# Weight signs from a two-slope ReLU on ScalarE, and a sum-of-squares bound for the weights, in an attention and MLP kernel

## The chip, the cores and the metric

The kernel runs on one core of one Trainium2 chip. The metric is the device time of one execution in microseconds (us). The core has a TensorE (PE; its weight loads are shown apart as PEld), a VectorE (DVE), a ScalarE (ACT), a GpSimd (POOL) and a SyncE (SP) that issues most of the DMAs.

## The reference

Attention over 4 batches of 8 heads, 768 positions of 64 numbers, in which a query sees only the keys of its own hash bucket; then a two-layer MLP with the ELU function between its layers. The MLP's weights reach the kernel as 64-bit floating-point numbers.

```python
q_bucket = np.sum((einsum(q, proj) > 0) * 2**arange(6), -1)      # k_bucket likewise
scores = np.where(q_bucket == k_bucket, q @ k.T / 8, -1e9)
attn = exp(scores - max) ; attn /= attn.sum() + 1e-9
x = (attn @ v)                      # 3072 tokens x 512
h = x @ w_in                        # w_in 512 x 2048
g = np.where(h > 0, h, exp(min(h, 0)) - 1)
out = g @ w_out                     # w_out 2048 x 512
```

## The kernel before

**Numbers in two halves.** Each matrix product runs on 16-bit operands. A 32-bit tensor is scaled by a power of two and split into a high half (helper `scaled`, line 143 when ScalarE does it) and the remainder (helper `rest`, line 152, on VectorE). Three matmuls then stand for one product: high by high, high by low and low by high. The power of two comes from a bound on the tensor, which `powers` (line 174) turns into an exponent `ex` and a scale `sc`. With `rows=True` the bound is already the same on each partition; without it, `powers` first adds the partitions up with a small matmul against the matrix `ones`, into a PSUM tile of pool `ps_a` (line 184). With `squares=True` the bound is a sum of squares, whose exponent is halved (lines 191 to 194, two VectorE instructions where the plain way has one, line 196).

**Weights.** `w_in` and `w_out` make 32 tiles of 128 x 512, 16 each. `wload` (line 444) loads a tile as pairs of 32-bit words (512 KB) into a ring of three places in `U` and one at the end of `W`. `wdecode` (line 460) makes 32-bit floats of it. The upper word `hi` of a 64-bit number, read as a 32-bit float and multiplied by 2^-112 on ScalarE (line 467, recorded at line 143), has its exponent where a shift left by 3 on VectorE (line 468) puts it right; the shift also pushes the sign out. Line 469 (VectorE) brings in three bits of the lower word `lo`. Then a matmul (line 472) of `ones` with the upper 16-bit halves of the tile adds its columns into the PSUM tile `acc`; while the sign is out, these are sums of magnitudes. At last line 479 (VectorE) takes the sign bit from `hi` and puts it in place. After the last tile of each matrix, line 477 reduces `acc` to its greatest entry, `wscale` (line 485) makes the scale, and `wsplit` (line 491) makes the 16-bit halves, which overwrite `W` in place. They are the tiles `w0s` (for `w_in`) and `w1s` (for `w_out`) in the profile.

**Attention.** The work goes by slots: 8 chunks (half a batch each) of 4 head pairs, 6 slots to a pair. A slot is 128 queries of one head against all 768 keys: `scores` (line 504) issues four matmuls and a VectorE instruction (line 520) that copies the scores out of PSUM and takes the maximum of each row; `exps` (line 528) does two slots' exponentials on ScalarE (line 536); `splits` (line 541) makes halves (lines 143 and 152, tile `hl`) and a DMA turns them over (line 551, tile `PT`). After a pair, `attend` (line 553) issues 36 matmuls into a `ps_a` tile, the pool's single buffer, and makes `x16`. `prep_k`, `prep_q` and `prep_v` load, scale and turn over the inputs ahead of their slots.

**MLP.** `moe_stream` (line 575) runs `first` (line 580: twelve matmuls into `h`, line 588, then ELU and the halves of `g`) and `second` (line 610: nine matmuls into `o`, line 624) for each chunk and each of 16 column groups. It can't begin before the first chunk's four `attend` calls and the `w_in` halves.

**What sets the order.** The loop over slots (line 894) issues scores, exponentials, MLP steps, input preparation and up to six weight steps (`weights(W_RATE)`, line 924) for each slot. A weight step is a `wdecode`, a `wsplit` or nothing, if the space of `W` is still in use by early inputs or if a load hasn't been issued. The framework's scheduler then sets each engine's order from its own forecast of times; from slot 30 on (`starts[0]`), TensorE's order is that of the program. Each engine executes its instructions in the order of its queue.

Of the kernel before, what the change touches and what calls it, by code (L numbers as in the profile page):

```python
# [9 lines left out]
BF16 = mybir.dt.bfloat16  # L10
F32 = mybir.dt.float32
I32 = mybir.dt.int32
AF = mybir.ActivationFunctionType
ALU = mybir.AluOpType
# [6 lines left out]
W_TOP = 13  # L21
# [30 lines left out]
    "n_lo": ("V", "V"),  # L52
    "v_hi": ("A", "A"),
    "v_lo": ("V", "V"),
    "w_mul": ("A", "A"),
    "w_sgn": ("V", "V"),
    "w_hi": ("A", "A"),
    "w_lo": ("V", "V"),
    "g_hi": ("A", "A"),
# [7 lines left out]
def lsh_attention_moe(  # L67
# [10 lines left out]
    nc = tc.nc  # L78
# [4 lines left out]
    P = 128  # L83
# [6 lines left out]
    FG = 4  # L90
    SL = FG * P
    NSI = (NF // FG) * KT
    NSO = NF
# [3 lines left out]
    const = ctx.enter_context(tc.tile_pool(name="const", bufs=1))  # L97
# [34 lines left out]
    def engine(kind):  # L132
        rest = int(now[0] > 0)
        n = turns.get((kind, rest), 0)
        turns[kind, rest] = n + 1
        names = ENGINES[kind][rest]
        return names[n % len(names)]

    def scaled(kind, o, x, s):

        e = engine(kind)
        if e == "A":
            nc.scalar.activation(o, x, AF.Copy, scale=s)  # L143
        elif e == "V":
            nc.vector.tensor_scalar(o, x, s, None, ALU.mult)
        else:
            nc.gpsimd.tensor_scalar(o, x, s, 1.0, ALU.mult, ALU.mult)
# [18 lines left out]
    ones = const.tile([P, P], BF16, name="ones")  # L166
# [7 lines left out]
    def powers(mx, n, floor, top, tag, pool=None, rows=False, squares=False, ex=None):  # L174

        pool = pool or small  # L180
        mall = pool.tile([P, n], F32, tag=tag + "m", name=tag + "m")
        if not rows:
            t = ps_a.tile([P, 512], F32, tag="av", name="sum")[:, :n]
            nc.tensor.matmul(t, ones, mx.bitcast(BF16).rearrange("p (n t) -> p n t", t=2)[:, :, 1], start=True, stop=True)
            mx = t
        nc.vector.tensor_scalar(mall, mx, floor, None, ALU.max)
        if ex is None:
            ex = pool.tile([P, n], F32, tag=tag + "e", name=tag + "e")
        if squares:

            nc.vector.tensor_scalar(
                ex.bitcast(I32), mall.bitcast(I32), 1, 0x7F800000, ALU.logical_shift_right, ALU.bitwise_and
            )
            nc.vector.tensor_scalar(ex, ex, 2.0**64, None, ALU.mult)
        else:
            nc.vector.tensor_scalar(ex.bitcast(I32), mall.bitcast(I32), 0x7F800000, None, ALU.bitwise_and)
        sc = pool.tile([P, n], F32, tag=tag + "s", name=tag + "s")
        nc.vector.reciprocal(sc, ex)
        nc.vector.tensor_scalar(sc, sc, 2.0**top, None, ALU.mult)
        return ex, sc  # L200
# [226 lines left out]
    wst = {}  # L427
# [32 lines left out]
    def wdecode(i):  # L460

        t = w64.pop(i)
        d = W[:, i + (2 if i >= NSI else 1), :]
        di = d.bitcast(I32)
        lo, hi = t[:, :, 0], t[:, :, 1]

        scaled("w_mul", d, hi.bitcast(F32), 2.0**-112)
        nc.vector.tensor_scalar(di, di, 3, None, ALU.logical_shift_left)
        nc.vector.scalar_tensor_tensor(di, lo, 29, di, ALU.logical_shift_right, ALU.bitwise_or)  # L469

        o = int(i >= NSI)
        nc.tensor.matmul(  # L472
            wst["acc"], ones, d.bitcast(BF16).rearrange("p (n t) -> p n t", t=2)[:, :, 1],
            start=i == o * NSI, stop=i in (NSI - 1, NSI + NSO - 1),
        )
        if i in (NSI - 1, NSI + NSO - 1):
            nc.vector.tensor_reduce(wst["m2"][:, o : o + 1], wst["acc"], axis=AX.X, op=ALU.max)
        if engine("w_sgn") == "V":
            nc.vector.scalar_tensor_tensor(di, hi, -(2**31), di, ALU.bitwise_and, ALU.bitwise_or)
        else:  # L480
            sign = hi.bitcast(F32)
            nc.scalar.activation(sign, sign, AF.Sign)
            nc.gpsimd.tensor_tensor(d, d, sign, ALU.mult)

    def wscale(o):
        wst["ex", o], wst["sc", o] = powers(wst["m2"][:, o : o + 1], 1, 2.0**-17, W_TOP, f"w{o}", const, rows=True)
        if o == 1:
            wst["e2"] = const.tile([P, 1], F32, name="we2")
            nc.vector.tensor_tensor(wst["e2"], wst["ex", 0], wst["ex", 1], ALU.mult)
# [244 lines left out]
    last = {}  # L734
# [3 lines left out]
    for ns in groups:  # L738
# [3 lines left out]
        for n in ns:  # L742
            at = begin[n] - (PREP0 if early else PREP)[2]

            w = 2 * chunks[pairs[n][0]]["nc"]
# [20 lines left out]
        for i, n in enumerate(ns):  # L766
# [7 lines left out]
            last = {"split": a, "project": z_last}  # L774
# [64 lines left out]
    def weights(n):  # L839
        nonlocal w_credit, w_at  # L840
        w_credit += n
        while w_credit >= 1:

            at = (w_at + (2 if w_at >= NSI else 1)) * SL
            users = {x[1] for x in due} | ({"v"} if len(vdue) == NP + 2 + (B - 1) * (2 * NP + 3) else set())
            if any(a < at + SL and at < z and users & u for a, z, u in guards):
                break
            if w_at not in w64 and w_at < NSI + NSO:
                break
            w_credit -= 1  # L850
            if w_at >= W_SPLIT and NSI not in split_done and len(split_done) < KT:
                split_w()
            elif w_at < NSI + NSO:
                wdecode(w_at)
                w_at += 1
                load_w()
                if w_at in (NSI, NSI + NSO):
                    wscale(w_at // (NSI + NSO))
            elif wq and (wq[0] if wq[0] < NSI else (wq[0] - NSI) // FG * KT) // KT <= moe_at[0] // FG + 1:
                split_w()  # L860
            else:
                break
# [31 lines left out]
    for G in range(starts[-2] + 1):  # L894
        if G == starts[0]:
            ordered.enter_context(tc.manual_schedule(engines={mybir.EngineType.PE}))
        if G < len(slots):
            n, at = slots[G]
            c = chunks[pairs[n][0]]
            b, p, j, t = c["b"], pairs[n][1], at // c["nc"], at % c["nc"]  # L900
# [59 lines left out]
```

## Time and profile before

| | before |
|---|---|
| median of 3 runs | 952.3 us (950.54 to 952.47) |
| span of the profiled execution | 952.0 us |
| TensorE busy | 817.4 us, 86% |
| VectorE busy | 703.4 us, 74% |
| ScalarE busy | 741.4 us, 78% |
| GpSimd busy | 15.7 us, 2% |
| mean granted TensorE clock | 0.958 |

A slice row of the profile cuts the span into 40 equal pieces of 23.8 us, and each digit is an engine's busy share in tenths. A row of a group gives the line of the kernel, the engine, the operation, output and input tiles with their shapes, the count, and then the busy time, the mean duration in ns of one, and the idle time of the engine just before such instructions with what ended it. A row of a stretch gives its start and end, its length, each engine's busy time and count, the granted clock (1.00 is full), the DMA engines' mean share and the rate in GB/s. Lines 143 and 152 belong to helpers, so the tile names tell the groups apart. The DMA share adds up the time that packets took, so it can pass 1.

### The profile page before, as it was taken

The numbers are of one execution on the slowest core, as the hardware profiler recorded it, in microseconds if no ns is written. First come the engines' busy times: TensorE is split into PE (matmuls) and PEld (weight loads), VectorE is DVE, ScalarE is ACT, GpSimd is POOL, SyncE is SP. The second block draws the span as 40 slices with busy tenths as digits, with TensorE's granted clock in tenths as the row PEclk, the third lists the DMA queues.
The fourth block names the chain that finished last, engine by engine and source line by source line (L and its number), as shares of the span: only waits on it lengthen the run. The fifth ranks groups of instructions, "written<-read, shape, count | busy, mean of one in ns | idle before, by whom it ended". The sixth has DMA issues, their size and how long they took to land.

```text
span 952.0 us, 14531 instructions
## 1 busy us (share of the span) xinstructions
PE 817.4 (86%) x4975; PEld 420.6 (44%) x4975; DVE 703.4 (74%) x1524; ACT 741.4 (78%) x1473; POOL 15.7 (2%) x49
## 2 busy tenths in 40 slices
PE   2445555987999999988998999998989999999996
PEld 0112222544545555544554455544445555555553
DVE  6798999887877867678776686787877687764332
ACT  5578876988979878789779787889888788885442
POOL 1000000000000000000000000000000000000000
PEclk9998656999999999999999999999999999999998
DMA  9999898676787768687887758795786767556000
GB/s 284 237 225 217 224 252 170 118 142 145 148 164 166 149 113 140 129 184 120 161 182 135 138 110 148 150 185 102 140 148 130 123 118 150 101 100 100 34 1 35
DMA packets 404587, 138.48 MB, mean 145 GB/s; under 512 B 380960, under 2 KB 398880, under 8 KB 404512
## 3 DMA queue, kind: packets, MB, share of 16 engines
q1 hardware_dynamic: 402432, 131.25, 69.5%
q0 software_dynamic: 1920, 6.29, 1.9%
q8 instruction: 39, 0.64, 0.3%
q14 instruction: 36, 0.29, 0.1%
q10 hardware_dynamic: 160, 0.00, 0.0%
HBM read 35.65 MB, written 6.29 MB: 44 GB/s over the span
## 4 chain that ended last, share of the span: by engine, by line
issue 77%; PE 11%; DMA 5%; DVE 3%; ACT 2%; POOL 1%; POOLq 0%; ACTq 0%; DVEq 0%
PE o L624 3%; PE h L588 3%; PE av L559 2%; PE s L508 2%; DMA K<-natk 1%; DMA O<-nat1q 1%; DMA out_dram<-W 1%; POOL out_dram L638 1%; ACT pt L536 1%; DVE pt L520 1%; DVE hl L152 1%; DMA PT<-hl 1%; DMA vf<-in_v_dram 0%; DVE natk L152 0%; ACT hl L143 0%
## 5 line engine op out<-in xcount | busy, mean ns | idle before, releaser
L624 PE MATMUL o<-W,U 128*128 128x512 f16 x1152 | 280.3, 379 | 4.3 <-ACT W L143 4.2
L588 PE MATMUL h<-x,W 128*128 128x384 f16 x1536 | 280.8, 327 | 0.8 <-ACT x L568 0.6
L588 PEld LDWEIGHTS <-W 128*128 128x128 f16 x1536 | 147.7, 98 | 112.6 <-issue 11.9
L536 ACT ACTIVATE pt<-pt,nb,sg 128x768 f32<-128x768 f32 x192 | 195.3, 1019 | 1.7
L152 DVE SCALAR_TENSOR_TENSOR hl<-pt,r,hl 128x768 f16<-128x768 f32 x192 | 189.5, 1012 | 8.8 <-ACT hl L143 8.4
L143 ACT ACTIVATE hl<-pt,r 128x768 f16<-128x768 f32 x192 | 168.4, 926 | 22.4 <-DVE r L546 22.0
L520 DVE TENSOR_SCALAR_CACHE_REDUCE pt<-s 128x768 f32<-128x768 f32 x177 | 168.1, 949 | 21.8 <-PE s L508 20.7
L508 PE MATMUL s<-K,O 128*128 128x384 f16 x708 | 153.8, 341 | 32.1 <-DVE pt L520 31.7
L624 PEld LDWEIGHTS <-U 128*128 128x128 f16 x1152 | 111.0, 98 | 125.4 <-issue 11.7
L559 PE MATMUL av<-PT,vhl 128*64 128x384 f16 x1152 | 113.8, 347 | 27.1 <-DMA PT<-hl 16.7
L603 DVE SCALAR_TENSOR_TENSOR U<-U 128x384 f32<-128x384 f32 x128 | 71.0, 555 | 86.7 <-ACT U L602 85.7
L508 PEld LDWEIGHTS <-O 128*128 128x128 f16 (+1 forms) x768 | 74.9, 102 | 129.9 <-issue 55.0
L152 DVE SCALAR_TENSOR_TENSOR U<-U,sgg 128x384 f16<-128x384 f32 x128 | 78.4, 612 | 59.7 <-ACT U L143 59.7
L599 ACT ACTIVATE U<-h,ch 128x384 f32<-128x384 f32 x128 | 72.9, 569 | 62.5 <-PE h L588 62.3
L559 PEld LDWEIGHTS <-vhl 128*64 128x64 f16 x1152 | 73.0, 116 | 73.5 <-ACT W L143 13.2
L143 ACT ACTIVATE U<-U,sgg 128x384 f16<-128x384 f32 x128 | 77.8, 608 | 19.9 <-DVE U L603 19.8
L602 ACT ACTIVATE U<-h,ch 128x384 f32<-128x384 f32 x128 | 73.0, 570 | 0.0
L472 PE MATMUL acc<-W,ones 128*128 128x512 bf16 x32 | 17.1, 554 | 33.9 <-DVE W L469 33.9
L536 ACT ACTIVATION_READ_ACCUMULATOR pt<-pt,nb,sg 128x1 f32 x192 | 36.3, 189 | 0.0
L533 ACT ACTIVATE nb<-m,sg 128x2 f32<-128x2 f32 x96 | 27.7, 288 | 8.7 <-DVE pt L520 8.7
L207 ACT ACTIVATE nat1q<-qst 128x384 bf16<-128x384 f32 x30 | 15.5, 517 | 18.9 <-DMA O<-nat1q 18.1
L291 DVE TENSOR_SCALAR zb<-z,pjt 64x384 f16<-64x384 f32 (+1 forms) x48 | 29.1, 606 | 1.2 <-PE z L286 1.2
(102 smaller groups left out, 527.2 us busy)
## 6 DMA issues: line engine op xcount, KB each, us to landing
U<-in_moe_w_in_dram SPq DMA_DIRECT2D x12, 512.0 KB
vf<-in_v_dram SPq DMA_DIRECT2D x16, 384.0 KB
U<-in_moe_w_out_dram SPq DMA_DIRECT2D x12, 512.0 KB
out_dram<-W POOLq DMA_DIRECT2D x24, 256.0 KB, 4.0
qst<-in_q_dram SPq DMA_DIRECT2D x30, 192.0 KB
kst<-in_k_dram SPq DMA_DIRECT2D x14, 384.0 KB
PT<-hl SPq DMA_TRANSPOSE x192
W<-in_moe_w_in_dram SPq DMA_DIRECT2D x4, 512.0 KB
```

The lines of the kernel that those rows point to most:

```text
L143: nc.scalar.activation(o, x, AF.Copy, scale=s)
L152: nc.vector.scalar_tensor_tensor(o, x, s, hi, ALU.mult, ALU.subtract)
L291: nc.vector.tensor_scalar(zb[used], t[used], pj["thr"][used, which : which + 1], (MBIT, -MBIT)[which], ALU.is_gt, ALU.mult)
L508: nc.tensor.matmul(s_tile[:, n, :HALF], st[o][:rows, at, :], kst[kk][:rows, j * NC + n * HC : j * NC + (n + 1) * HC, :].rearrange("p a b - ...
L520: top = nc.vector.tensor_scalar(pt.rearrange("p (n e) -> p n e", n=2), s_tile[:, :, :HALF], CLAMP, None, ALU.max, ALU.max, accum_out=duo[0 ...
L536: nc.scalar.activation(pt, pt, AF.Exp, bias=nb[:, n : n + 1], scale=st["sg"][:, 0:1], accum_out=sm[:, n : n + 1])
L559: nc.tensor.matmul(av[j * D : (j + 1) * D], vt[:, j, c, vx, :], PTs[j][:, :, px, c, :], start=n == 0, stop=n == last,)
L588: nc.tensor.matmul(h, WH[:, g * KT + t, wx, fc * P : (fc + 1) * P], c["xs"][t][:, xx, :], start=n == 0, stop=n == 3 * KT - 1,)
L599: nc.scalar.activation(e, h, AF.Exp, scale=c["ch"])
L602: nc.scalar.activation(hp, h, AF.Relu, scale=c["ch"])
L603: nc.vector.scalar_tensor_tensor(e, e, -1.0, hp, ALU.add, ALU.min)
L624: nc.tensor.matmul(o[t][:, :DO], g16[:, gx, t * P : (t + 1) * P], WH[:, NSI + 1 + f, wx, :], start=f == 0 and i == 0, stop=f == NF - 1 and ...
```

## The change

The first step of `wdecode` becomes a ReLU with a slope for negative inputs (`Prelu`). A positive word is multiplied by 2^-112 as before. A negative word is multiplied by 2^-112 and by -(2^32): it comes out positive with an exponent that is greater by 32, and the shift left by 3 moves that bit of the exponent to the place of the sign. So the float has its sign after line 469, and the VectorE instruction of line 479 is gone, and with it the last reading of the upper words after the ScalarE step.

The tile has its signs when the bound is taken, so a sum of the columns no longer bounds it. In place of one matmul of `ones` with 512 columns, each tile now has four matmuls, each of a 128 x 128 block of the upper halves with itself, whose diagonal holds the sums of squares of the block's columns. The maximum over `acc` is taken as before. It differs from partition to partition, so `wscale` calls `powers` without `rows`, which adds the small matmul with `ones` into a `ps_a` tile, and with `squares`, which has one more VectorE instruction. Both happen once for each matrix.

```diff
-    "w_mul": ("A", "A"),
-    "w_sgn": ("V", "V"),
...
-        scaled("w_mul", d, hi.bitcast(F32), 2.0**-112)
+        nc.scalar.activation(d, hi.bitcast(F32), AF.Prelu, scale=2.0**-112, alpha=-(2.0**32))
         nc.vector.tensor_scalar(di, di, 3, None, ALU.logical_shift_left)
         nc.vector.scalar_tensor_tensor(di, lo, 29, di, ALU.logical_shift_right, ALU.bitwise_or)
         o = int(i >= NSI)
-        nc.tensor.matmul(
-            wst["acc"], ones, d.bitcast(BF16).rearrange("p (n t) -> p n t", t=2)[:, :, 1],
-            start=i == o * NSI, stop=i in (NSI - 1, NSI + NSO - 1),
-        )
-        if i in (NSI - 1, NSI + NSO - 1):
+        top = d.bitcast(BF16).rearrange("p (n t) -> p n t", t=2)[:, :, 1]
+        last = i in (NSI - 1, NSI + NSO - 1)
+        for u in range(FG):
+            x = top[:, u * P : (u + 1) * P]
+            nc.tensor.matmul(
+                wst["acc"][:, u * P : (u + 1) * P], x, x,
+                start=i == o * NSI and u == 0, stop=last and u == FG - 1, skip_group_check=True,
+            )
+        if last:
             nc.vector.tensor_reduce(wst["m2"][:, o : o + 1], wst["acc"], axis=AX.X, op=ALU.max)
-        if engine("w_sgn") == "V":
-            nc.vector.scalar_tensor_tensor(di, hi, -(2**31), di, ALU.bitwise_and, ALU.bitwise_or)
-        else:
-            sign = hi.bitcast(F32)
-            nc.scalar.activation(sign, sign, AF.Sign)
-            nc.gpsimd.tensor_tensor(d, d, sign, ALU.mult)
     def wscale(o):
-        wst["ex", o], wst["sc", o] = powers(wst["m2"][:, o : o + 1], 1, 2.0**-17, W_TOP, f"w{o}", const, rows=True)
+        wst["ex", o], wst["sc", o] = powers(wst["m2"][:, o : o + 1], 1, 2.0**-34, W_TOP, f"w{o}", const, squares=True)
```

## The prediction

> **What bounds the kernel now.** I read the page first, its slices above all, then a table of busy time by stretches, whose cuts I chose from the slices.
>
> ```profile
> span 952.0 us, 14531 instructions
> PE   2445555987999999988998999998989999999996
> DVE  6798999887877867678776686787877687764332
> PEclk9998656999999999999999999999999999999998
> ```
> ```profile
> 0.00:40.00 40.00, 10.42 (x39) 2.34 (x39) 26.19 (x89) 20.19 (x38) 2.57 (x25) 1.00 0.99 279
> 40.00:90.00 50.00, 28.36 (x127) 11.05 (x126) 45.76 (x120) 36.95 (x74) 0.00 (x0) 1.00 0.93 218
> 90.00:170.00 80.00, 45.11 (x210) 19.80 (x211) 75.13 (x155) 63.50 (x123) 0.00 (x0) 0.60 0.88 204
> 170.00:260.00 90.00, 79.32 (x489) 41.08 (x488) 76.70 (x166) 81.06 (x162) 0.00 (x0) 0.96 0.74 142
> 260.00:930.00 670.00, 640.39 (x4046) 339.68 (x4045) 475.35 (x991) 533.32 (x1069) 11.52 (x21) 1.00 0.68 129
> ```
>
> In each stretch the columns after its length are PE, PEld, DVE, ACT and POOL busy, then clock, DMA share and rate. The reader is to see two kernels in one span. From 260 to 930 us PE is busy 640.39 of 670: that part lasts as long as TensorE needs, and nothing that the change touches lies in it. Before 170 PE is half idle and DVE is the full engine: 45.76 of 50 and 75.13 of 80. In 0 to 40 DVE has only 26.19 of 40, and the DMA share is 0.99. So what VectorE sheds before 170 is worth time, more in the third stretch than in the first, and every microsecond by which the MLP starts earlier ends the kernel as much earlier. All weight tiles are decoded in that early part:
>
> ```profile
> L588 PE MATMUL h<-x,W x1536: 323/326/527, 169.9 to 937.6; 128*128 128x384 f16 x192
> L624 PE MATMUL o<-W,U x1152: 376/379/634, 179.1 to 943.4; 128*128 128x512 f16 x192
> L469 DVE SCALAR_TENSOR_TENSOR W<-U,W x24: 670/682/693, 13.4 to 157.1; 128x512 int32<-128x512 int32 x24
> ```
>
> The first `h` matmul starts at 169.9 and the last decoding step of line 469 at 157.1.
>
> **Removed: the sign step.** Two groups hold line 479, and the stretches tell where it runs.
>
> ```profile
> L479 DVE SCALAR_TENSOR_TENSOR W<-U,W 128x512 int32<-128x512 int32 x24 | 16.4, 682 | 0.7 <-PE acc L472 0.7
> L479 DVE SCALAR_TENSOR_TENSOR W<-W 128x512 int32<-128x512 int32 x8 | 5.5, 682 | 0.1
> ```
> ```profile
> 0.00:40.00 40.00, 6.14 (x9) 1.00 0.99 279
> 40.00:90.00 50.00, 5.42 (x8) 1.00 0.93 218
> 90.00:170.00 80.00, 10.24 (x15) 0.60 0.88 204
> ```
>
> 32 steps of 682 ns are 21.8 us of VectorE, and that is the most that can be gained. I credit each stretch apart. In 0 to 40 the first attention slots wait for inputs that come by DMA; DVE idles 13.8 us, and a shorter DVE mostly idles longer. Of 6.14 I take 1, with 0 and 4.0 as ends (4.0 is 6.14 by DVE's busy share of 26.19 in 40). In 40 to 90 DVE is 92% busy; of 5.42 I take 3.3. In 90 to 170 it is 94% busy, and the slots' chain runs through it; of 10.24 I take 7, because the DMA share of 0.88 leaves 80 - 70.4 = 9.6 us by which that stretch can shrink before the same packets fill it. Sum: 11.3, ends 0 and the whole 21.8.
>
> What comes late next is the turning over of `hl` (DMA), then `attend`: after line 152's last `hl` of a pair come a transfer and 36 matmuls, and no weight step shortens these. That is why I take two thirds and not all.
>
> **Moved: the ring place comes free sooner.** Line 479 was the last reader of a loaded tile, now it is line 469. The weight loads wait for it on SP's queue, where the transposes stand behind them.
>
> ```profile
> SPq L456 <- DVE W L479: 8.5, 7, 2.8
> DVE W L468 <- ACT W L143: 3.9, 8, 0.8
> DVE zb L291 <- PE z L286: 1.0, 2, 0.7
> DVE W L479 <- PE acc L472: 0.7, 1, 0.7
> PE acc L472 <- DVE W L469: 33.9, 15, 6.5
> ```
>
> Seven loads waited 8.5 us in all for the sign step. They will be issued one VectorE step earlier, 0.7 us or more each. They then meet the transposes a little earlier, in stretches with a DMA share of 0.88 to 0.99. ACT's wait for weights isn't on the path to the slots, so I count 0, with -1 (loads out of the transposes' way) and +2 (in their way) as ends.
>
> **Changed: the scaling step on ScalarE.** The trace has no such ReLU with a slope.
>
> ```profile
> L143 ACT ACTIVATE W<-U 128x512 f32<-128x512 f32 x24 | 15.7, 663 | 14.5 <-DMA U<-in_moe_w_in_dram 7.8 <-DMA U<-in_moe_w_out_dram 6.6
> L143 ACT ACTIVATE W<-W,w0s 128x512 f16<-128x512 f32 x16 | 11.3, 709 | 2.2 <-DVE W L152 2.2
> L602 ACT ACTIVATE U<-h,ch 128x384 f32<-128x384 f32 x128 | 73.0, 570 | 0.0
> L599 ACT ACTIVATE U<-h,ch 128x384 f32<-128x384 f32 x128 | 72.9, 569 | 62.5 <-PE h L588 62.3
> L207 ACT ACT_TABLE_LOAD x1 | 1.3, 1283 | 2.0 <-issue 2.0
> ```
>
> The plain scaling of such a tile takes 663 ns, one whose scale comes from a tile 709; Exp (line 599) and ReLU (line 602) of one shape take 569 and 570, so the function sets no price here. I take 663, hence nothing; the other end is 709, 32 x 46 ns = 1.5 us of an engine that is busy 120.6 of 170 us. Nothing below nothing: the element count is the same. One row more matters: the only table load of the whole trace, 1283 ns. It returns as a rival.
>
> **Changed: the bound.** Per tile one weight load and one matmul of 512 columns become four of each with 128 columns. The trace has no such matmuls, so I go by pace, in three rows: consecutive weight loads of the score matmuls (384 columns each) under a half clock, and two full-clock runs of the MLP.
>
> ```profile
> 157.02 0.15 PEld L508 LDWEIGHTS <-O 128*128 128x128 f16 x1 [0.17 <-issue]
> 157.34 0.15 PEld L508 LDWEIGHTS <-O 76*128 76x128 f16 x1 [0.17 <-issue]
> ```
> ```profile
> 305.51 1.94 PE o L624 x9
> 308.11 1.95 PE h L588 x12
> ```
>
> At full clock 512 columns take 1.94/9 = 0.216 us, 384 take 0.163; at half clock 384 take 0.32, so 512 would take 0.43. Four pairs with a weight load each cost no less than the same 512 columns, and no more than four of the 384 kind: 0.216 to 0.65 us a tile at full clock, 0.43 to 1.28 at half. The extra is 0 to 0.43 and 0 to 0.85. The Trainium skill speaks against the change here: "TensorE: Matmul & The Clock Gate", section "Back-to-back issue gap", puts a stream of loads and matmuls at about 81 ns a matmul for 128 columns and 131 for 512, so by it the estimate is 324 against 131, 0.19 us more a tile; the trace's 0.216 for 512 is not its 131. With all 32 tiles on the path the sum would lose some 6 us by it, an estimate.
>
> What lies beside it: PE is idle 21.6 of 50 and 34.9 of 80 us, much of it in front of this very matmul (33.9 us for line 469). Behind it in PE's queue stand the scores, for which line 520 waits; but the list of DVE's waits before 170 has no wait for scores, and the greatest for PE is 1.0 (line 291). So DVE has scores in hand. I count 1 us on the path. If that cover is gone, the whole extra counts: 17 tiles before 90 us at up to 0.43 and 15 after at up to 0.85, 20.1 us.
>
> **Added: one small matmul and a wait, twice.**
>
> ```profile
> L184 PE MATMUL sum<-vx,ones 128*128 128x1 bf16 x4 | 0.7, 177 | 1.4 <-DVE x L569 1.4
> L194 DVE TENSOR_SCALAR ve<-ve 128x1 f32<-128x1 f32 x4 | 0.6, 146 | 0.0
> ```
> ```profile
> 160.23 0.68 DVE L477 TENSOR_REDUCE wm<-acc 128x1 f32<-128x512 f32 x1
> 163.24 0.15 DVE L186 TENSOR_SCALAR w1m<-wm 128x1 f32<-128x1 f32 x1
> 164.45 4.89 PE L559 MATMUL av<-PT,vhl 128*64 128x384 f16 x35 [0.55 <-DMA PT<-hl]
> ```
>
> The matmul is 177 ns and the instruction 146 ns. The matmul waits for line 477 and for the one `ps_a` buffer; behind it in PE's queue stand scores and `attend`, and `powers` on DVE waits for it. For `w_out` the reduction is at 160.23, line 186 at 163.24: 2.3 us of slack lie between them already. If it lands behind an `attend`, the scale comes up to 4.9 us later; the `w_out` halves aren't read before 179.1. I count 0.3 us, ends 0 and 5.
>
> **Sum.** 11.3 - 1 - 0.3 = 10 us off the span of 952.0, so 942.0. The span is 0.3 below the median of 952.3, so the forecast of the median is 942.3. On the way the scheduler gets other durations and may set another order on DVE and ACT; the trace can't price that, and I let it widen the range by a few us.
>
> **The rivals.** *DVE's gain in full.* If the DMA packets' time is mostly waiting for one another (the share of 0.99 in the first stretch holds 279 GB/s, 0.88 holds 204), DMA yields, and up to 21.8 us go: 930.5. For it: DVE near 94% busy; against: the idle 13.8 us of the first stretch, and the transfers at each pair's end. Chance 0.12 for 935 or less.
>
> *DMA holds the start.* The transposes and loads of 170 us have a share that adds up to 0.99 x 40 + 0.93 x 50 + 0.88 x 80 = 156.5 us. If they can't be packed closer, DVE's freed time turns into waits for `PT` and `K`, and the gain is 2 or less: 950 to 953. Against it: pauses in the share and DVE's few waits for DMA. Chance 0.08.
>
> *TensorE takes DVE's place.* At half clock (0.60 in the third stretch) each decode puts four loads and matmuls ahead of scores, in order. From the point where the extra on the path passes the 0.68 us that DVE saves per tile, the change loses; at the upper price of 0.85 a tile it does. With the whole 20.1 us on the path and the forecast's credit of 11.3: 952.3 + 8.8 = 961. Against it: PE's idle time above. Chance 0.05.
>
> *The slope function isn't in the loaded table.* Then it needs one table load, and the next Exp one back. If it happened for each of 32 tiles, 64 x 1.283 = 82 us of ACT; it has 170 - 120.6 = 49 free, so at least 33 us are over: about 975 with the credit of 10, and more with less. Once per few tiles would still eat ScalarE's slack. One load in this trace serves squares, Copy, Exp and ReLU. The Trainium skill, "ScalarE: Activation LUTs", section "Table sets: the hidden batching unit", names relu, copy and abs as filler in every set, and doesn't name this function; no run here shows it yet. Chance 0.03.
>
> **How the numbers follow.** The forecast with its own range of 935 to 950 has 0.72, and the rivals 0.12, 0.08, 0.05 and 0.03. About 0.2%, 1.9 us, is what can be told from no change, so "same" is 950.4 to 954.2. Faster gets 0.72 + 0.12 and a small part of the third, 0.85; same 0.07; slower 0.08. The range goes from 930 to 953: it leaves out some 0.04 below (an order that happens to fit better) and 0.1 above.
>
> **What would show it.** Line 479 gone, DVE's sum 21 us lower, its busy share before the first `h` about as high; first `h` near 160; the pace after 260 unchanged; still one table load; ACT's scaling at 663 ns; four matmuls per tile and DVE without waits for scores. I am wrong if the first `h` stays near 169.9, or if it moves and the end doesn't follow: then the stretch after it, where PE had 79.32 of 90, swallowed the gain.

## The result, and the profile after

The changed kernel takes 965.1 us (964.06 to 967.44), the kernel before 952.4 in the same comparison: a ratio of 1.0132, with a 95% interval of 1.0105 to 1.0159. It is slower by 12.8 us, where 10 us faster was forecast. The span of the profiled execution is 962.3 us.

VectorE did shed its work: the steps of line 479, 32 of 0.68 us, are gone. Its busy time went from 703.4 to 688.3 us, 15.1 less, where the prediction had 21; records that overlap count once in the busy time. First the page of the changed kernel, with its slices, then its stretches (length, PE, PEld, DVE, ACT and POOL busy, clock, DMA share, rate).

```profile
span 962.3 us, 14700 instructions
PE   2445346798898999899999999998989999999996
DVE  5687887778787768587877767787878687774332
PEclk9999557799999999999999999999999999999998
```
```profile
0.00:40.00 40.00, 10.85 (x70) 5.07 (x71) 22.48 (x82) 20.12 (x37) 2.58 (x25) 1.00 0.97 281
40.00:90.00 50.00, 24.56 (x106) 10.74 (x106) 42.55 (x115) 39.87 (x80) 0.00 (x0) 1.00 0.88 209
90.00:170.00 80.00, 41.92 (x246) 23.54 (x244) 64.22 (x128) 57.88 (x105) 0.00 (x0) 0.64 0.71 175
```

The reader is to see that no engine is full before 170 any more. In the third stretch DVE fell from 75.13 to 64.22 of 80 us, no longer near full, and the DMA share fell from 0.88 to 0.71: something keeps all of them waiting. The next rows, by tile, are the changed kernel's.

```profile
L587 PE MATMUL h<-x,W x1536: 322/326/337, 187.1 to 948.2; 128*128 128x384 f16 x192
L477 PE MATMUL acc<-W x128: 269/308/314, 11.7 to 143.4; 128*128 128x128 bf16 x128
L469 DVE SCALAR_TENSOR_TENSOR W<-U,W x24: 668/686/694, 13.2 to 142.4; 128x512 int32<-128x512 int32 x24
```

The decoding ends at 142.4 and not at 157.1, so it did get faster. But the first `h` comes at 187.1 and not at 169.9, 17.2 us later. What `h` waits for is attention, and TensorE's order shows where it stood (changed kernel, timeline of PE):

```profile
85.50 0.16 PE L182 MATMUL sum<-wm,ones 128*128 128x1 bf16 x1 [1.80 <-DVE wm L482]
89.15 5.31 PE L558 MATMUL av<-PT,vhl 128*64 128x384 f16 x36 [0.71 <-DVE zb L289]
...
143.15 0.61 PE L477 MATMUL acc<-W 128*128 128x128 bf16 x4 [0.59 <-DVE W L469]
144.54 0.16 PE L182 MATMUL sum<-wm,ones 128*128 128x1 bf16 x1 [0.78 <-DVE wm L482]
144.95 4.73 PE L558 MATMUL av<-PT,vhl 128*64 128x384 f16 x36 [0.25 <-DVE w1m L184]
```

Here are the same `attend` groups before:

```profile
79.64 4.63 PE L559 MATMUL av<-PT,vhl 128*64 128x384 f16 x35 [2.30 <-DMA PT<-hl]
93.66 0.48 PE L559 MATMUL av<-PT,vhl 128*64 128x384 f16 x1 [0.70 <-DVE zb L291]
106.77 4.41 PE L559 MATMUL av<-PT,vhl 128*64 128x384 f16 x32 [1.54 <-ACT hl L143]
```

The second `attend` began its bulk at 106.77 before; now it begins at 144.95, right behind the new small matmul (line 182) for `w_out`, and what released it is line 184, the instruction that reads that matmul's result out of PSUM. The small matmul stands behind the last weight tile (143.15). So a pair of heads, whose last transpose was issued by about 106 us (SP's queue below), waited for the last weight tile. The first `attend` is held up in the same way, with a step between: behind the small matmul for `w_in` a matmul of the input preparation (`z`, also a `ps_a` tile) has its turn, `zb` (line 289) reads it out, and then comes `attend`.

Why it has to, as I read it (theory A below): the pool `ps_a` has one buffer, and its tiles get it in the order in which the program asks for it. The program decodes ahead: by its own order of issue the 32nd tile and the `w_out` scale are in slot 13, and the second `attend` in slot 15. Before, nothing tied the two, and the scheduler put the `attend` between weight tiles. With a `ps_a` tile in `powers`, `attend` stands behind the small matmul, and that behind all the weights.

And why it starves the rest: `PT` has two buffers, one for each head of the pair. Until `attend` has read them, no `hl` can be turned over. SP's queue (changed kernel) has these two entries for `PT`, and no other between them:

```profile
94.43 11.83 SPq L550 DMA_TRANSPOSE PT<-hl  x6
149.65 10.55 SPq L550 DMA_TRANSPOSE PT<-hl  x6
```

Between 106 and 145 us DVE is busy 32.95 of 39 us at a DMA share of 0.72. The row of before for the same cut had 38.42 and 0.96:

```profile
106.00:145.00 39.00, 15.76 (x82) 7.84 (x79) 32.95 (x69) 27.26 (x51) 0.00 (x0) 0.50 0.72 230
```
```profile
106.00:145.00 39.00, 24.20 (x125) 11.17 (x125) 38.42 (x78) 30.50 (x58) 0.00 (x0) 0.64 0.96 227
```

Of the 17.2 us, 10.3 are left at the end of the span. About half of the rest comes back in the first 40 us of the MLP, in which TensorE is now busy 37.93 us and was 34.64. As I read it, that is because the `w_out` halves, which used to be made there, were made while attention stood still (145.7 to 183.3, before 169.0 to 223.6).

### The profile page after: what moved, and what is told of

It reads as the page before. It is cut to its first block, busy times and chain, and to the rows that moved or that the text cites. A ratio compares the mean times of both kernels' runs of the same rounds, so it can differ in the third digit from the quotient of the medians.

```text
span 962.3 us, 14700 instructions
## 1 busy us (share of the span) xinstructions
PE 820.7 (85%) x5073; PEld 430.9 (45%) x5073; DVE 688.3 (72%) x1494; ACT 744.8 (77%) x1473; POOL 15.7 (2%) x49
## 4 chain that ended last, share of the span: by engine, by line
issue 49%; DMA 16%; PE 14%; DVE 10%; ACT 8%; SPq 2%; POOL 1%; POOLq 0%; ACTq 0%; DVEq 0%
DMA PT<-hl 4%; PE o L623 3%; PE av L558 3%; ACT pt L535 3%; PE h L587 3%; PE s L507 3%; DMA O<-nat1q 3%; DVE pt L519 2%; DMA K<-natk 2%; DVE hl L150 2%; DMA U<-in_moe_w_out_dram 2%; DMA K<-W 2%; ACT hl L141 1%; POOL out_dram L637 1%; DMA kst<-in_k_dram 1%
## 5 line engine op out<-in xcount | busy, mean ns | idle before, releaser
L141 ACT ACTIVATE hl<-pt,r 128x768 f16<-128x768 f32 x192 | 168.9, 927 | 24.7 <-DVE r L545 22.2
L507 PEld LDWEIGHTS <-O 76*128 76x128 f16 (+1 forms) x768 | 75.3, 102 | 135.3 <-issue 72.0
L558 PEld LDWEIGHTS <-vhl 128*64 128x64 f16 x1152 | 75.1, 117 | 57.6 <-DMA PT<-hl 14.2
L477 PE MATMUL acc<-W 128*128 128x128 bf16 x128 | 19.4, 305 | 40.1 <-DVE W L469 38.4
L507 PE MATMUL so<-K,O 128*128 128x384 f16 (+1 forms) x60 | 21.1, 492 | 23.7 <-DVE pt L519 23.6
L477 PEld LDWEIGHTS <-W 128*128 128x128 bf16 x128 | 11.7, 131 | 52.2 <-DVE W L469 47.6
```

The lines of the kernel that those rows point to most:

```text
L477: nc.tensor.matmul(wst["acc"][:, u * P : (u + 1) * P], x, x, start=i == o * NSI and u == 0, stop=last and u == FG - 1, skip_group_check=True,)
L507: nc.tensor.matmul(s_tile[:, n, :HALF], st[o][:rows, at, :], kst[kk][:rows, j * NC + n * HC : j * NC + (n + 1) * HC, :].rearrange("p a b - ...
L558: nc.tensor.matmul(av[j * D : (j + 1) * D], vt[:, j, c, vx, :], PTs[j][:, :, px, c, :], start=n == 0, stop=n == last,)
```

## The experiments

Theory A is the turn in `ps_a`, as told. Theory B is the prediction's rival that TensorE takes DVE's place, with four loads and matmuls per tile at a half clock. Theory C is that a shorter decode makes the scheduler put weights ahead of attention. Times are medians of all runs. The ratio is against the kernel before on the same chip, with its 95% interval, and needn't be the ratio of the medians; the last column is the ratio less 1, times 952.4, and differences between runs below go by it.

| run | us | ratio (95%) | us against before |
|---|---|---|---|
| the change | 965.1 | 1.0132 (1.0105 to 1.0159) | +12.6 |
| e1, sum in acc | 940.4 | 0.9886 (0.9863 to 0.9909) | -10.9 |
| e2, before and the small matmul | 971.1 | 1.0205 (1.0186 to 1.0223) | +19.5 |
| e3, signs only | 945.6 | 0.9931 (0.9906 to 0.9956) | -6.6 |
| e4, sums behind the attends | 949.5 | 0.998 (0.9954 to 1.0007) | -1.9 |
| e5, bound only, sum in acc | 952.7 | 0.9985 (0.9962 to 1.0008) | -1.4 |
| e6, first sum in acc | 958.2 | 1.0044 (1.0024 to 1.0064) | +4.2 |
| e7, second sum in acc | 948.4 | 0.994 (0.992 to 0.996) | -5.7 |
| e8, sums in ps_h | 940.0 | 0.9856 (0.9828 to 0.9884) | -13.7 |
| e9, second sum behind the fourth attend | 933.0 | 0.9796 (0.975 to 0.9841) | -19.4 |
| e10, before with a late scale | 954.3 | 1.0029 (1.0011 to 1.0047) | +2.8 |
| e11, sum in acc with a late scale | 940.3 | 0.988 (0.9855 to 0.9904) | -11.4 |

**e1: the small matmul out of the queue.**

```diff
-            t = ps_a.tile([P, 512], F32, tag="av", name="sum")[:, :n]
+            t = into if into is not None else ps_a.tile([P, 512], F32, tag="av", name="sum")[:, :n]
...
-        ... = powers(wst["m2"][:, o : o + 1], 1, 2.0**-34, W_TOP, f"w{o}", const, squares=True)
+        ... = powers(wst["m2"][:, o : o + 1], 1, 2.0**-34, W_TOP, f"w{o}", const, squares=True, into=wst["acc"][:, :1])
```

> The changed kernel, but the small matmul that adds the partitions up writes column 0 of the tile acc, which line 482 has just read, and takes no ps_a buffer. Theory A (the small matmul takes its turn in the one ps_a buffer ahead of the second attend, so attend waits for the last weight tile): the second attend is back near 107 us, the first h comes at 160 to 168, the time is 940 to 948. Theory B (four loads and matmuls per weight tile hold TensorE at half clock): 961 to 967, as changed. Theory C (with a shorter decode the scheduler puts weights ahead of attention): 960 to 966.

940.4 us, 12.6 + 10.9 = 23.5 less than the changed kernel, with the same instructions. In its timeline the second `attend` begins its bulk at 97.44, and the first `h` is at 158.1 (rows of e1):

```profile
97.44 5.45 PE L558 MATMUL av<-PT,vhl 128*64 128x384 f16 x35 [0.46 <-DMA PT<-hl]
```
```profile
L587 PE MATMUL h<-x,W x1536: 322/326/527, 158.1 to 926.9; 128*128 128x384 f16 x192
```

The time fits A, and both events came earlier than A had said (107 and 160 to 168). B and C are out by more than 19 us, since both the four matmuls and the shorter decode are still there.

**e2: only the small matmul, in the kernel before.**

```diff
+    mean = const.tile([P, P], BF16, name="mean")
+    nc.gpsimd.memset(mean, 2.0**-7)
...
-        ... = powers(wst["m2"][:, o : o + 1], 1, 2.0**-17, W_TOP, f"w{o}", const, rows=True)
+        ... = powers(wst["m2"][:, o : o + 1], 1, 2.0**-17, W_TOP, f"w{o}", const, by=mean)
```

> The kernel before with one addition: after each matrix's reduction a small matmul with a matrix of 1/128 into a ps_a tile (the bound stays as it was). Signs, ReLU and the ones matmul are those of before. Theory A: the second attend waits for the last weight tile, which before came at 157, so the first h comes 10 to 25 us later and the time is 960 to 975. Theories B and C: two matmuls of 0.2 us, 951 to 954.

971.1 us, 19.5 more than before, for two matmuls of 0.2 us and none of the rest of the change. The first `h` comes at 193.2, 23.3 us later than before. The rows of e2 are the same picture:

```profile
150.04 0.16 PE L186 MATMUL sum<-wm,mean 128*128 128x1 bf16 x1 [0.78 <-DVE wm L479]
150.71 4.49 PE L561 MATMUL av<-PT,vhl 128*64 128x384 f16 x36 [0.50 <-DVE w1m L188]
```

So the harm needs neither the four matmuls nor the faster decode.

**e3: only the signs.**

```diff
-        for u in range(FG):
-            x = top[:, u * P : (u + 1) * P]
-            nc.tensor.matmul(wst["acc"][:, u * P : (u + 1) * P], x, x, ...)
+        nc.tensor.matmul(wst["acc"], ones, top, start=i == o * NSI, stop=last)
```

> The ReLU with a slope and no line 479, but the old bound: one matmul of ones with 512 columns, rows=True, no small matmul. The bound is then taken of signed column sums, which bounds nothing in general. Theory A: all of the gain, 936 to 946. Theory B: the same. Theory C: 958 to 966, since the shorter decode is all that is left.

945.6 us, in A's range and out of C's. It has the first `h` at 154.3, before e1's 158.1, and yet gains 4 us less than e1. None of its four runs (943.56 to 947.22) reaches down to e1's (939.15 to 942.74), so the difference is likely real. It arises after the first `h`: from 170 to 260 TensorE is busy 79.44 us in e3 and 82.61 in e1. Its cause is open.

**e4: the same tiles, asked for a few slots later.** The calls of `wscale` are put in a list and made behind `run_attend`; a half whose scale isn't there yet is not issued.

```diff
-                    wscale(w_at // (NSI + NSO))
+                    late.append(w_at // (NSI + NSO))
...
             run_attend(*waiting.pop(0)[1])
+            while late:
+                wscale(late.pop(0))
```

> The changed kernel, small matmul still in ps_a, but the two calls of wscale are issued in the program behind the first and the second attend (slots 9 and 15) and not ahead of them (slots 6 and 13). Theory A: the attends no longer wait, second attend by 115, 940 to 950. Theory B: 961 to 967. Theory C: 960 to 966. If the sum's buffer alone counts and not its turn, the third attend would wait in place of the second: 952 to 965.

949.5 us. The time alone would fit A's 940 to 950, but A's reason doesn't hold for all of it. The second `attend` is free, and the third one has its turn behind the `w_out` sum, with a `z` of the input preparation between, and waits in its place (rows of e4):

```profile
97.77 3.48 PE L558 MATMUL av<-PT,vhl 128*64 128x384 f16 x35
144.29 0.16 PE L182 MATMUL sum<-wm,ones 128*128 128x1 bf16 x1 [0.78 <-DVE wm L482]
145.02 1.26 PE L284 MATMUL z<-O,pjz 128*32 128x384 f16 x6 [0.56 <-DVE w1m L184]
147.10 3.17 PE L558 MATMUL av<-PT,vhl 128*64 128x384 f16 x20 [0.82 <-DVE zb L289]
```

In e1 the third began its bulk at 130.61. So the last sentence of the expectation came true, if a little below its range of 952 to 965: the turn moves with the place in the program.

**e5: only the bound.** The plain scaling and line 479 of before, the four matmuls and `squares=True` of after, the sum in `acc` as in e1.

> The kernel before with its plain scaling and its sign step of line 479, but with the new bound: four matmuls of 128 columns per weight tile, and the small matmul into acc and not into ps_a. It prices the four matmuls alone. If they cost the 1 us that the prediction counted: 951 to 954. Theory B, four loads and matmuls on the path at 0.19 to 0.85 us a tile: 957 to 972.

952.7 us, the kernel before within its interval. The four matmuls per tile and the small ones cost nothing that can be measured once the turn is out of the way; B is refuted. And e1 differs from e5 by the signs alone (the ReLU, and line 479 gone), so these are worth 10.9 - 1.4 = 9.5 us, or 12.3 by the two medians; with intervals of about 2 us on each run, the two figures don't contradict each other.

**e6 and e7: one sum each.** e6 has `into=wst["acc"][:, :1] if o == 0 else None`, e7 the same with `o == 1`.

> The changed kernel with the small matmul of w_in in acc, that of w_out still in ps_a. Theory A: the second attend still waits for the last weight tile at about 144, so most of the loss is left: 955 to 966.

> The changed kernel with the small matmul of w_out in acc, that of w_in still in ps_a. Theory A: only the first attend waits, for the sixteenth tile at about 85, which is 5 to 10 us of delay: 940 to 950.

958.2 and 948.4 us, each in its range. Against e1 the turn of `w_out` costs 4.2 + 10.9 = 15.1 us and that of `w_in` 10.9 - 5.7 = 5.2, in sum 20.3; both together, in the changed kernel, cost 23.5, which the intervals of about 2 us on each side allow. By medians they are 17.8, 8.0 and 24.7. In e6 the second `attend` begins at 134.46, behind the sum at 133.58; in e7 the first begins at 89.40, behind the sum at 85.75, where e1 had the bulk of it at 77.28.

**e8: another pool.** `into=ps_h.tile([P, 512], F32, tag="h", name="sum")[:, :1]`.

> The changed kernel with both small matmuls into a tile of the pool ps_h, whose two buffers nothing uses before the first h. If only the turn in ps_a counts, this is like the run with the sum in acc: 937 to 945. If writing into acc gained something of its own (or lost it by holding up the next matrix's first matmul), the two differ by more than 3.

940.0 us, like e1: 0.4 us apart by the medians, 2.8 by the ratios, whose intervals overlap. So it isn't `acc` that helps.

**e9: the last turn.** `w_in`'s sum in `acc`; `w_out`'s in `ps_a`, issued behind the fourth `attend`.

```diff
-                    wscale(w_at // (NSI + NSO))
+                    wscale(0) if w_at == NSI else late.append(1)
...
+            n, _ = waiting[0][1]
             run_attend(*waiting.pop(0)[1])
+            if late and n == NP - 1:
+                wscale(late.pop(0))
```

> The changed kernel with the small matmul of w_in in acc; that of w_out stays in ps_a, but is issued in the program behind the fourth attend (slot 27) and not in slot 13, so that no attend of the first chunk has its turn behind it. Theory A (the turn decides, not the pool or the matmul): the second attend is back before 100 us and the first h before 165, and the time is 938 to 950; the w_out halves come later, which may take some of the gain. If a matmul and its buffer in ps_a cost something apart from the turn: 953 or more.

933.0 us, below the 938 to 950 that I had expected, and the fastest version of the study: 2% below the kernel before. A's claim holds (the turn decides: second `attend` at 97.51, first `h` at 156.4). For what it gains beyond e1, 8.5 us by the ratios (its own interval is about 4 us to each side) and 7.4 by the medians, I made two more runs.

**e10 and e11: is it the later scale?** e10 is the kernel before, e11 is e1, both with e9's later call.

> The kernel before, with the w_out scale (line 485, second call) issued in the program behind the fourth attend and not in slot 13; nothing else. The run with the second sum behind the fourth attend was some 7 us faster than the one with the sum in acc. If that came from the later scale as such (fewer w_out halves among the last slots, first o earlier): 943 to 949 here. If it belongs to the changed kernel's order alone: 951 to 955.

> The changed kernel with both small matmuls in acc and the w_out scale issued behind the fourth attend. If the later scale as such gave the 7 us: 930 to 937. If the ps_a tile behind the fourth attend gave it: 938 to 943.

954.3 and 940.3 us: the later call as such gains nothing, and in the kernel before it costs 2.8 us. So the gain goes with the `ps_a` tile behind the fourth `attend`. As I read the traces, it is again the turn, this time in the kernel's favour. e11 makes the first `w_out` halves before it has read out the fourth `attend` (`x`, lines 567 and 568), and `h` waits for `x`:

```profile
154.01 0.71 ACT L141 ACTIVATE W<-W,w1s 128x512 f16<-128x512 f32 x1
...
159.69 0.47 ACT L567 ACTIVATE x<-av 128x384 f16<-128x384 f32 x1
160.21 0.32 PE L587 MATMUL h<-x,W 128*128 128x384 f16 x1 [1.53 <-ACT x L567]
...
161.65 0.55 DVE L568 SCALAR_TENSOR_TENSOR x<-av,x 128x384 f16<-128x384 f32 x1
```

e9 can't do so, since its sum has its turn behind that `x`:

```profile
157.07 0.47 ACT L567 ACTIVATE x<-av 128x384 f16<-128x384 f32 x1
158.69 0.56 DVE L568 SCALAR_TENSOR_TENSOR x<-av,x 128x384 f16<-128x384 f32 x1
159.30 0.18 PE L182 MATMUL sum<-wm,ones 128*128 128x1 bf16 x1 [1.08 <-DVE x L568]
...
162.62 0.71 ACT L141 ACTIVATE W<-W,w1s 128x512 f16<-128x512 f32 x1
```

The first `o` is at 165.7 in e9 and at 170.3 in e11. That is 4.6 of the 8 us between e9 and e11; it is read from the two traces and wasn't tried by itself, and the remainder is open.

## Why the prediction was wrong, point by point

- **What bounds the kernel: right before the first `h`, not behind it.** The signs are worth 9.5 us (e5 against e1; 12.3 by medians) with the new bound and 6.6 with the old one (e3), where the sum had 11.3 from three stretches. With the turn out of the way, e1's 940.4 us is close to the forecast of 942.3. But the prediction took every microsecond of an earlier first `h` to be one at the end, and that doesn't hold: the first `h` moved by 14.6 us, from 172.7 in e5 to 158.1 in e1, and the span by 10.9, from 951.8 to 940.9. In e3 it came 15.6 us earlier than before and the span fell by 6.6, and in the changed kernel it came 17.2 later and the span grew by 10.3. So it is in part luck that the sum of 11.3 comes so close: the early part gained more than that, and the part behind it gave some back.
- **The scaling step: right.** In the changed kernel it takes 668 and 659 ns where 663 and 661 stood before, and there is still one table load:

```profile
L467 ACT ACTIVATE W<-U 128x512 f32<-128x512 f32 x24 | 15.9, 668 | 14.7 <-DMA U<-in_moe_w_in_dram 8.8 <-DMA U<-in_moe_w_out_dram 5.8
L467 ACT ACTIVATE W<-W 128x512 f32<-128x512 f32 x8 | 5.3, 659 | 5.9 <-DMA W<-in_moe_w_in_dram 4.1 <-DMA W<-in_moe_w_out_dram 1.9
L205 ACT ACT_TABLE_LOAD x1 | 1.3, 1283 | 2.0 <-issue 2.0
```

  The function is in the loaded set, and the rival of 0.03 is out.
- **The four matmuls: right in size.** I counted 1 us; by e5's interval they cost at most 0.8. By the prediction's estimate of 0.19 us a tile, from the figures of the Trainium skill ("TensorE: Matmul & The Clock Gate", section "Back-to-back issue gap"), 6 us would have been lost with all of it on the path. e5 shows no such loss, and the rows in the last section show no such extra.
- **The added matmul and its wait: here it failed.** The step is "Added: one small matmul and a wait, twice". The prediction named the one `ps_a` buffer, and then asked only how late the sum would come "if it lands behind an `attend`", and counted "0.3 us, ends 0 and 5". It did not ask what lands behind the sum. Two entries are put into a queue of one, and the second of them waits for the last weight tile; the price is that wait, 144.95 - 106.77 = 38 us of a late `attend`, of which some 15 us reach the end; the first `attend`, behind `w_in`'s sum, adds some 5. Together they measure 23.5 us. The 10.9 that e1 gains less these 23.5 is the 12.6 by which the change is slower.
- **What misled:** I read the slack from 160.23 to 163.24, in which the old scale was made, as cover for the wait. That is cover for who uses the scale; the `attend` isn't one of those. The program's order (wscale in slot 13, `attend` in slot 15) could be worked out from the kernel's loops, and the trace of before showed the inversion: the second `attend` ran at 106.77, and the last weight tile's matmul at 158.7, so an order that ties the `attend` to the latter had to delay it by tens of microseconds.
- **The rivals.** None had this cause. Of the two that ended slower, the table load did not happen, and "TensorE takes DVE's place" had the right engine and the wrong reason: TensorE stood still, but in front of one matmul and not because of many. "DMA holds the start" is out by e1: it gained 10.9 us, with a DMA share of 0.97 from 90 to 170 where the kernel before had 0.88, so the packets could be packed closer.

## What to carry to other kernels

Before a new tile is drawn from a pool with one buffer, list who draws from it in the order of the program, and compare that with the times at which the trace shows them: if the newcomer is ready later than the one behind it, the one behind can be late by that difference, however short the newcomer is (here 38 us, of which some 15 reached the end). A helper's flag (`rows`) can hide such a draw. A place that is read out already, like `acc` here, costs no turn.

## What the runs showed that I had not expected

Four loads and matmuls of 128 columns take no longer than one of 512 here. At a granted clock of 0.50 two tiles together take 1.06 us either way, as four and four in e5 (first row) and as one and one in the kernel before (second row).

```profile
160.82 1.06 PE L476 MATMUL acc<-W 128*128 128x128 bf16 x8
```
```profile
158.30 1.06 PE L472 MATMUL acc<-W,ones 128*128 128x512 bf16 x2
```

And the granted clock of the early part tells little of the time: e1 had 0.64 in its stretch from 40 to 90, where the kernel before and the changed one had 1.00, and was faster than both. e8 had 0.98 there and took 940.0 us, e1 940.4. So TensorE's clock isn't what the time of that stretch hangs on.
